# Memory attention, tanhshrink and maxout on one core: g three steps ahead instead of two

## The chip, the core and the metric

The kernel runs on one core of one Trainium2 chip. The time is device microseconds (us) of one execution. A core has TensorE (PE, matmuls), VectorE (DVE), ScalarE (ACT), GpSimd (POOL) and SyncE (SP), which issues most of the DMAs; each works through its own queue of instructions in order, and they wait for one another through semaphores.

## The reference

All inputs come as 64-bit floats. There are 8 batches of 576 tokens, 4608 tokens in all, with 8 heads of width 64.

```python
a = softmax(phi, axis=seq)                       # phi: 32 memory slots per head
k_m, v_m = a^T k, a^T v                          # 32 x 64 per head
x = softmax(q k_m^T / 8) v_m                     # back to 4608 x 512
h = x @ w_in                                     # 512 -> 2048
g = h - tanh(h)
x2 = g @ w_out                                   # 2048 -> 512
m = max(x2 @ w1, x2 @ w2, x2 @ w3)               # 512 -> 768
out = m @ w_out2                                 # 768 -> 512
```

## The kernel before

Every product is made of three matmuls on pairs (the value rounded to the matmul's format, and the rest), by the helper `mm3` (lines 93 to 96). So every weight is first split into such a pair from its 64-bit input by `conv` (lines 116 to 143): one ScalarE step, five VectorE steps, then POOL and ScalarE for the two halves.

Attention and the first layer are merged. For each batch, `phi_gen` and `kv_mm` build the memory keys and values, `vw_gen` multiplies the memory values with a quarter of w_in into the weight tile `vw`, and `q_gen` gives the attention probabilities `at`. h is then the product of `vw` and `at`.

The main loop has 200 steps in two phases, each phase with half of the 2048 inner columns. A step is one chunk of 128 inner columns (8 to a phase) for one tile of 288, 320 or 512 tokens; a tile of 512 spans two batches. `emit_h` computes h of a step into one of two PSUM banks, `emit_g` applies tanh (ScalarE, line 453), subtracts from h in PSUM (VectorE, line 454), rounds (ScalarE, line 456) and takes the rest (POOL, line 457) into a tile `gh`. `emit_x` multiplies `gh` with a chunk of w_out and adds up in four PSUM banks; the last step of a tile adds or copies them to `xo` (lines 485 and 487) and stores that. `LG` is the lookahead: while step i is multiplied, g of step i + LG is made after the first quarter of the products, and h of step i + LG + 1 after the last.

Attention, weight conversion and the like stand in two tracks, `fg` and `bg`, one after another in each. `slot()`, called five times per step, takes some pieces from each; a piece can have a gate, the step from which it may be taken. If `emit_h` or `emit_x` needs something that isn't out yet, `need` empties the track up to it. This gives the order of emission. The order in which an engine really executes comes from the framework's scheduler, which runs a timeline of its own and prefers what was emitted first among what is ready; a thing can run long before or after its neighbours in the code.

After the two phases comes the last stage: nine tiles of 512 tokens. For each, `emit_max` makes six chunks j of the three maxout products (216 matmuls in all) with weights `wb[j]`, and `emit_out` multiplies the maxima with w_out2 (72 matmuls). `wb[0]` and `wb[1]` are converted during phase 1, stored to DRAM, and loaded (line 611) into the pool `pre`, which takes the room of phase 0's w_out. `wb[2]` is loaded the same way (line 631) into the pool `wb`, which takes the room of the two phases' tiles; `wb[3]` to `wb[5]` and the six `wz` are converted while the first tiles of the stage run.

Of the kernel before, what the change touches and what calls it, by code (L numbers as in the profile page):

```python
# [7 lines left out]
F32 = mybir.dt.float32  # L8
F32R = mybir.dt.float32r
# [13 lines left out]
def kernel(  # L23
# [23 lines left out]
    V, S, G, T, DMA = nc.vector, nc.scalar, nc.gpsimd, nc.tensor, nc.sync  # L47
    B, H, NS, D = q.shape
    M = phi.shape[3]
    P = 128  # L50
# [6 lines left out]
    KD = DM // P  # L57
    FQ = 512
    NT = 512
    NX = B * NS // NT  # L60
    LG = 2
    AHEAD = 20
    FC = 8
    J = 6

    def pool(name, space=None, stack=ctx, **kw):
        if space is not None:
            kw["space"] = space
        if space is not DRAM:
            kw["reuse_waits"] = "tile"  # L70
        return stack.enter_context(tc.tile_pool(name=name, bufs=1, **kw))
# [8 lines left out]
    ga_p = pool("ga", stack=main)  # L80
    cv_p = pool("cv", stack=main)
    at_p = pool("at", stack=main)
    attn = ExitStack()
    ap = pool("attn", stack=attn)
# [5 lines left out]
    def f(x):  # L90
        return x.bitcast(F32)

    def mm3(o, w, x, start, stop):
        T.matmul(o, w[0], x[0], start=start, stop=False)  # L94
        T.matmul(o, w[0], x[1], start=False, stop=False)  # L95
        T.matmul(o, w[1], x[0], start=False, stop=stop)  # L96
# [5 lines left out]
    def bank(i, shape, name):  # L102
        return ps_m.tile(shape, F32, tag=f"m{i}", bufs=1, name=name)
# [11 lines left out]
    def conv(src, hi, lo=None):  # L115
        raw = cv[0].tile([P, 512, 2], U32, tag="raw", bufs=2, name="raw")
        u = src.bitcast(U32)
        DMA.dma_start(out=raw.rearrange("p (k c) t -> p k (c t)", k=u.shape[1]) if len(u.shape) == 3 else raw.rearrange("p c t -> p (c t)"), in_=u)
        yield
        yield  # L120
        a = cv[0].tile([P, 512], U32, tag="cva", bufs=2, name="cva")
        b = cv[0].tile([P, 512], U32, tag="cvb", bufs=2, name="cvb")
        hw, lw = raw[:, :, 1], raw[:, :, 0]
        S.activation(f(a), f(hw), AF.Abs)
        yield
        V.tensor_scalar(f(a), f(a), TINY, HUGE, ALU.max, ALU.min)
        V.tensor_scalar(b, a, 3, 0x3FFFFFF8, ALU.logical_shift_left, ALU.bitwise_and)
        yield
        V.scalar_tensor_tensor(out=b, in0=hw, scalar=0xC0000000, in1=b, op0=ALU.bitwise_and, op1=ALU.bitwise_or)  # L129
        yield  # L130
        V.tensor_scalar(a, b, 0xFF800000, None, ALU.bitwise_and)
        V.scalar_tensor_tensor(out=f(a), in0=lw, scalar=2.0 ** -52, in1=f(a), op0=ALU.mult, op1=ALU.mult)
        yield
        if lo is None:
            G.tensor_add(hi, f(b), f(a))
            yield
            return
        G.tensor_add(f(a), f(b), f(a))
        x = f(a).rearrange("p (k c) -> p k c", k=hi.shape[1]) if len(hi.shape) == 3 else f(a)
        S.copy(hi, x)  # L140
        yield
        G.tensor_sub(lo, x, f(hi))  # L142
        yield
# [13 lines left out]
    def load_phi(b):  # L157
        if b < B and b not in phi_t:
            t = ap.tile([P, H, C, M], F32, tag="phi", bufs=1, name="phi")
            DMA.dma_start(out=t[:, :, :4], in_=phi[b, :, :4 * P].rearrange("h (p c) m -> p h c m", p=P))  # L160
            DMA.dma_start(out=t[:64, :, 4], in_=phi[b, :, 4 * P:].rearrange("h p m -> p h m"))
            G.memset(t[64:, :, 4], -3e38)
            phi_t[b] = t
# [22 lines left out]
    def phi_gen(b):  # L186
        load_phi(b)
        ph = phi_t.pop(b)
        yield
        mx = ap.tile([P, H, M], F32, tag="mx", bufs=1, name="mx")  # L190
        V.tensor_reduce(mx, ph.rearrange("p h c m -> p h m c"), axis=AX.X, op=ALU.max)
        yield
        pm = bank(1, [P, 2, 2, P], "ps_mx")
        for i in range(2):
            T.transpose(pm[:, 0, i], mx[:, 4 * i:4 * i + 4].rearrange("p h m -> p (h m)"), ident)
        mt = ap.tile([P, 2], F32, tag="mt", bufs=1, name="mt")
        V.tensor_reduce(mt, pm[:, 0], axis=AX.X, op=ALU.max)
        yield
        dg = ap.tile([P, 2, P], F32, tag="dg", bufs=1, name="dg")
        V.tensor_tensor(out=dg, in0=ident[:, None, :].to_broadcast([P, 2, P]), in1=mt[:, :, None].to_broadcast([P, 2, P]), op=ALU.mult)  # L200
        T.matmul(pm[:, 1].rearrange("p i j -> p (i j)"), ones, dg.rearrange("p i j -> p (i j)"), start=True, stop=True)
        yield
        freed[1] = V.tensor_tensor(out=ph, in0=ph, in1=pm[:, 1].rearrange("p i (h m) -> p (i h) m", m=M)[:, :, None, :].to_broadcast([P, H, C, M]), op=ALU.subtract).ins
        yield
        S.activation(ph, ph, AF.Exp)
        yield
        ph_t[b] = ph
        yield
# [39 lines left out]
    def kv_gen(b):  # L248
        yield from phi_gen(b)
        yield from kv_mm(b)  # L250
# [93 lines left out]
    JP = 3  # L344
    wb_d = [dram.tile([P, 3, KD, 2, P], F32, name=f"wb_d{j}") for j in range(JP)]

    def wb_conv(w, j, t=None):
        o = cv_p.tile([P, KD, 2, P], F32R, tag="cs", bufs=1, name="cs") if t is None else t[:, w]
        src = (moe2_w1, moe2_w2, moe2_w3)[w]
        yield from conv(src[:, j * P:(j + 1) * P].rearrange("(k p) c -> p k c", p=P), o[:, :, 0], o[:, :, 1])  # L350
        if t is None:
            DMA.dma_start(out=wb_d[j][:, w], in_=f(o))
            yield
# [34 lines left out]
    fg, bg = Track(), Track()  # L388
    now, cnt, rate = [0], [0], [10, 8]

    def slot():
        cnt[0] += 1
        for i, tr in enumerate((fg, bg)):
            for _ in range((cnt[0] * rate[i]) // 4 - ((cnt[0] - 1) * rate[i]) // 4):
                tr.step(now[0])
# [53 lines left out]
    def emit_g(i):  # L449
        ps = h_t.pop(i)  # L450
        nt = steps[i][1][1]
        th = ga_p.tile([P, NT], F32, tag="th", bufs=2, name="th")[:, :nt]
        S.activation(th, ps, AF.Tanh)  # L453
        V.tensor_sub(th, ps, th)  # L454
        gh = ga_p.tile([P, 2, NT], F32R, tag="gh", bufs=3, name="gh")[:, :, :nt]
        S.copy(gh[:, 0], th)  # L456
        G.tensor_sub(gh[:, 1], th, f(gh[:, 0]))  # L457
        g_t[i] = gh
# [6 lines left out]
    def emit_x(i):  # L465
# [13 lines left out]
        for dm in range(KD):  # L479
            mm3(emit_x.ps[dm], (wt[:, 0, dm * P:(dm + 1) * P], wt[:, 1, dm * P:(dm + 1) * P]),  # L480
                (gh[:, 0], gh[:, 1]), first, final)
            if final:
# [3 lines left out]
                else:  # L486
                    (S.copy if dm % 2 else V.tensor_copy)(xo[:, dm], ps)
            if dm == 0 and i + LG < len(steps):
                emit_g(i + LG)
            slot()  # L490
# [5 lines left out]
    def run(lo, hi):  # L496
        for i in range(lo, hi):
# [3 lines left out]
            emit_x(i)  # L501
            if i + LG + 1 < len(steps):
                emit_h(i + LG + 1)
            slot()
# [34 lines left out]
    for ph in range(2):  # L539
        for b in range(B):  # L540
            s0, bb = start[ph, b], ph * B + b
            order += [(bb, 0), (bb, 1)] if bb > 1 else []
            aq = max([s0 - AHEAD + 4] + [last_u[bb - 3, fq] - LG for fq in range(2) if bb > 2])
            av0, av1 = (max(s0 - d, last_u[order[2 * bb + fq - 4]] - LG) if bb > 1 else 0 for fq, d in enumerate((8, 6)))
            if ph == 0 and b > 1:
# [34 lines left out]
    wo_s.close()  # L580
    last = ExitStack()
    pre_p = pool("pre", stack=last, side="right")
    wb = [pre_p.tile([P, 3, KD, 2, P], F32R, name=f"wb{j}") for j in range(2)]
    x_t = {}
    xh_p = [pre_p]

# [20 lines left out]
    def pre():  # L607
        while bg.q:
            bg.step(10 ** 9)
        for j in range(2):  # L610
            G.dma_start(out=wb[j], in_=wb_d[j])
        load_x(0)

    hooks[start[2, 0] - 14] = [pre]
# [7 lines left out]
    wb_p = pool("wb", stack=last2)  # L622
# [2 lines left out]
    cv[0] = b_p  # L625
    ps_b = pool("ps_b", PSUM, last2)
    wz = []
    for j in range(2, J):
        wb.append(wb_p.tile([P, 3, KD, 2, P], F32R, name=f"wb{j}"))
        if j < JP:  # L630
            G.dma_start(out=wb[j], in_=wb_d[j])
        else:
            for w in range(3):
                bg.add(("wb", j), wb_conv(w, j, wb[j]))
    for j in range(J):
        wz.append(wb_p.tile([P, 2, DM], F32R, name=f"wz{j}"))
        bg.add("wz", wz_conv(j, wz[j]))
# [3 lines left out]
    def emit_max(i, j):  # L641
        xh = x_t[i]
        pss = []
        bg.need_all(("wb", j))
        for w in range(3):
            for _ in range(LR):
                bg.step(10 ** 9)
            ps = ps_b.tile([P, NT], F32, tag=f"w{w}", bufs=2, name=f"ps_w{w}")
            for kc in range(KD):
                mm3(ps, (wb[j][:, w, kc, 0], wb[j][:, w, kc, 1]), (xh[:, 0, kc], xh[:, 1, kc]), kc == 0, kc == KD - 1)  # L650
            pss.append(ps)
        m = b_p.tile([P, NT], F32, tag="m", bufs=2, name="m")
        S.copy(m, pss[0])
        V.tensor_max(m, pss[1], m)  # L654
        V.tensor_max(m, pss[2], m)
        mh = b_p.tile([P, 2, NT], F32R, tag="mh", bufs=12, name="mh")
        S.copy(mh[:, 0], m)  # L657
        G.tensor_sub(mh[:, 1], m, f(mh[:, 0]))  # L658
        m_t[i, j] = mh
# [59 lines left out]
```

## Time and profile before

| | us |
|---|---|
| median of 3 timed runs | 1469.13 |
| lowest and highest | 1468.34, 1474.32 |
| the profiled execution | 1464.11 |
| its span | 1462.4 |
| TensorE busy in it | 1359.7 |
| VectorE busy in it | 637.0 |
| POOL busy in it | 450.9 |
| ScalarE busy in it | 418.6 |

The span runs from the first to the last instruction that the profile shows. Durations are those of the one profiled execution. Matmuls overlap, so their pace is read from the distance of two starts and not from the duration of one. The first product of phase 1 starts at 524.0 us, phase 1 ends at 849 us, and the last stage takes the rest.

### The profile page before, as it was taken

The page shows a single profiled execution, that of the slowest core. Times are in us where ns is not written, and L with a number is a line of the kernel's source. Part 1 is how long each engine was busy: PE and PEld are TensorE (multiplying, and loading weights), DVE is VectorE, ACT ScalarE, POOL GpSimd, SP SyncE. Part 2 cuts the span into 40 slices and gives each one's busy share as a digit, 9 for nine tenths or more (in the row PEclk, how much of TensorE's full clock was granted, in tenths as well). Part 3 has the DMA queues.
Part 4 walks back from the last instruction along what each step waited for, and adds up shares of the span by engine and source line. Part 5 has one row for each costly group of instructions (what it writes and reads, how often), then busy time and mean ns, then how long its engine had stood idle before and what let it go on. Part 6 is the DMA issues. An engine that isn't in the chain of part 4 may idle for free.

```text
span 1462.4 us, 21348 instructions
## 1 busy us (share of the span) xinstructions
PE 1359.7 (93%) x8672; PEld 1128.9 (77%) x8672; DVE 637.0 (44%) x1013; ACT 418.6 (29%) x805; POOL 450.9 (31%) x399
## 2 busy tenths in 40 slices
PE   2576898999998999999999999899999999999998
PEld 1354786887886888888889987788888888888886
DVE  3889977446538773323223269621212121121110
ACT  1334334344334443433333233311111111111110
POOL 0446554334325663232223345511111111111110
PEclk9687999999999999999999999999999999999999
DMA  8565887535615583413221242210101011110001
GB/s 203 155 195 145 234 256 216 136 116 134 159 68 209 185 271 128 144 67 111 66 80 56 88 164 87 87 44 15 43 15 49 17 43 30 37 29 15 15 15 44
DMA packets 177970, 152.39 MB, mean 104 GB/s; under 512 B 94160, under 2 KB 153552, under 8 KB 176464
## 3 DMA queue, kind: packets, MB, share of 16 engines
q1 hardware_dynamic: 177440, 146.31, 33.5%
q0 software_dynamic: 432, 4.72, 1.0%
q8 instruction: 68, 1.11, 0.3%
q14 instruction: 30, 0.25, 0.1%
HBM read 101.97 MB, written 49.02 MB: 103 GB/s over the span
## 4 chain that ended last, share of the span: by engine, by line
PE 72%; DVE 12%; DMA 5%; SPq 4%; issue 3%; POOL 2%; ACT 1%; DVEq 0%; POOLq 0%; ACTq 0%
PE ps_w L96 9%; PE ps_w L95 9%; PE ps_w L94 9%; PE ps_x L94 7%; PE ps_x L95 7%; PE ps_x L96 7%; PE ps_h L94 4%; PE ps_h L96 4%; PE ps_h L95 4%; PE ps_o L95 3%; PE ps_o L96 3%; PE ps_o L94 3%; SPq L181 2%; PE ps_w L106 2%; DVE cvb L129 2%
## 5 line engine op out<-in xcount | busy, mean ns | idle before, releaser
L457 POOL TENSOR_TENSOR gh<-th,gh 128x320 fp32r<-128x320 f32 (+2 forms) x200 | 204.3, 1023 | 348.0 <-ACT gh L456 329.2
L95 PE MATMUL ps_x<-gh,wo 128*128 128x320 f32 (+2 forms) x800 | 267.4, 336 | 1.5 <-POOL gh L457 1.5
L94 PE MATMUL ps_x<-gh,wo 128*128 128x320 f32 (+2 forms) x800 | 255.4, 338 | 10.3 <-DVE xo L485 4.2
L96 PE MATMUL ps_x<-gh,wo 128*128 128x320 f32 (+2 forms) x800 | 263.9, 333 | 0.5 <-POOL wo L142 0.5
L94 PE MATMUL ps_w<-xh,wb 128*128 128x512 f32 x648 | 255.4, 394 | 3.5 <-ACT wb L140 3.5
L95 PE MATMUL ps_w<-xh,wb 128*128 128x512 f32 x648 | 255.7, 395 | 0.0
L96 PE MATMUL ps_w<-xh,wb 128*128 128x512 f32 x648 | 255.3, 395 | 0.0
L658 POOL TENSOR_TENSOR mh<-m,mh 128x512 fp32r<-128x512 f32 x54 | 71.5, 1324 | 446.0 <-ACT mh L657 445.9
L454 DVE TENSOR_TENSOR th<-ps_h,th 128x320 f32<-128x320 f32 (+2 forms) x200 | 106.9, 536 | 223.1 <-ACT th L453 222.8
L94 PEld LDWEIGHTS ps_x<-gh,wo 128*128 128x128 f32 x800 | 148.7, 191 | 37.4 <-issue 17.8
L94 PE MATMUL ps_h<-at,vw 128*128 128x320 f32 (+2 forms) x512 | 159.7, 313 | 18.0 <-ACT at L297 9.9
L95 PEld LDWEIGHTS ps_x<-gh,wo 128*128 128x128 f32 x800 | 152.4, 190 | 18.9 <-issue 7.2
L96 PEld LDWEIGHTS ps_x<-gh,wo 128*128 128x128 f32 x800 | 152.0, 190 | 11.0 <-issue 0.9
L96 PE MATMUL ps_h<-at,vw 128*128 128x320 f32 (+2 forms) x512 | 155.9, 306 | 1.5 <-DVE vw L317 1.5
L95 PE MATMUL ps_h<-at,vw 128*128 128x320 f32 (+2 forms) x512 | 155.8, 304 | 0.0
L453 ACT ACTIVATE th<-ps_h 128x320 f32<-128x320 f32 (+2 forms) x200 | 94.8, 477 | 208.5 <-PE ps_h L96 198.6
L94 PEld LDWEIGHTS ps_w<-xh,wb 128*128 128x128 f32 x648 | 122.5, 189 | 31.8 <-ACT wb L140 4.3
L456 ACT CAST gh<-th 128x320 fp32r<-128x320 f32 (+2 forms) x200 | 99.9, 500 | 162.7 <-DVE th L454 150.0
L654 DVE TENSOR_TENSOR m<-ps_w,m 128x512 f32<-128x512 f32 x54 | 37.3, 690 | 246.2 <-PE ps_w L96 246.2
L95 PEld LDWEIGHTS ps_w<-xh,wb 128*128 128x128 f32 x648 | 122.5, 189 | 27.9
L96 PEld LDWEIGHTS ps_w<-xh,wb 128*128 128x128 f32 x648 | 122.4, 189 | 27.6 <-POOL wb L142 0.3
L94 PEld LDWEIGHTS ps_h<-at,vw 128*128 128x128 f32 x512 | 100.4, 196 | 41.4 <-DVE th L454 17.1
(83 smaller groups left out, 1694.1 us busy)
## 6 DMA issues: line engine op xcount, KB each, us to landing
raw<-in_moe_w_out_dram SPq DMA_DIRECT2D x22, 512.0 KB, 3.4
qt<-in_q_dram SPq DMA_DIRECT2D x128, 72.0 KB, 2.8
at_d<-at SPq DMA_DIRECT2D x16, 576.0 KB, 3.5
at<-at_d SPq DMA_DIRECT2D x8, 1152.0 KB, 5.0
raw<-in_moe_w_dram SPq DMA_DIRECT2D x18, 512.0 KB, 3.6
xr<-xd SPq DMA_DIRECT2D x36, 256.0 KB, 2.8
out_dram<-ob SPq DMA_DIRECT2D x144, 64.0 KB, 1.7
xd<-xo SPq DMA_DIRECT2D x14, 640.0 KB, 3.5
```

Of the source, the lines that this page charges most:

```text
L94: T.matmul(o, w[0], x[0], start=start, stop=False)
L95: T.matmul(o, w[0], x[1], start=False, stop=False)
L96: T.matmul(o, w[1], x[0], start=False, stop=stop)
L106: ins = [T.matmul(o, w, x, start=True, stop=True).ins for o, w, x in mms]
L129: V.scalar_tensor_tensor(out=b, in0=hw, scalar=0xC0000000, in1=b, op0=ALU.bitwise_and, op1=ALU.bitwise_or)
L181: DMA.dma_start(out=t[64 * e + 32 * h:64 * e + 32 * h + 32, r], in_=src[e, h, r])
L453: S.activation(th, ps, AF.Tanh)
L454: V.tensor_sub(th, ps, th)
L456: S.copy(gh[:, 0], th)
L457: G.tensor_sub(gh[:, 1], th, f(gh[:, 0]))
L654: V.tensor_max(m, pss[1], m)
L658: G.tensor_sub(mh[:, 1], m, f(mh[:, 0]))
```

## The change

`LG` becomes 3, and `gh` gets four buffers in place of three. The diagonal tile `dg` of `phi_gen` takes the buffer of `mx`. The weights of the last stage become one tile for each j and each of the three products, (j, w), instead of one for each j. Five of them, (0, 0) to (1, 1), are loaded into `pre` in phase 1; (1, 2) is loaded at the start of the last stage, ahead of (2, 0) to (2, 2).

```diff
-    LG = 2
+    LG = 3
...
-        dg = ap.tile([P, 2, P], F32, tag="dg", bufs=1, name="dg")
+        dg = ap.tile([P, 2, P], F32, tag="mx", bufs=1, name="dg")
...
-        gh = ga_p.tile([P, 2, NT], F32R, tag="gh", bufs=3, name="gh")[:, :, :nt]
+        gh = ga_p.tile([P, 2, NT], F32R, tag="gh", bufs=4, name="gh")[:, :, :nt]
...
-    wb = [pre_p.tile([P, 3, KD, 2, P], F32R, name=f"wb{j}") for j in range(2)]
+    wb = {(j, w): pre_p.tile([P, KD, 2, P], F32R, name=f"wb{j}{w}") for j, w in ((0, 0), (0, 1), (0, 2), (1, 0), (1, 1))}
...
-        for j in range(2):
-            G.dma_start(out=wb[j], in_=wb_d[j])
+        for j, w in wb:
+            G.dma_start(out=wb[j, w], in_=wb_d[j][:, w])
...
-    for j in range(2, J):
-        wb.append(wb_p.tile([P, 3, KD, 2, P], F32R, name=f"wb{j}"))
-        if j < JP:
-            G.dma_start(out=wb[j], in_=wb_d[j])
-        else:
-            for w in range(3):
-                bg.add(("wb", j), wb_conv(w, j, wb[j]))
+    for j in range(1, J):
+        for w in range(3):
+            if (j, w) not in wb:
+                wb[j, w] = wb_p.tile([P, KD, 2, P], F32R, name=f"wb{j}{w}")
+                if j < JP:
+                    G.dma_start(out=wb[j, w], in_=wb_d[j][:, w])
+                else:
+                    bg.add(("wb", j), wb_conv(w, j, wb[j, w]))
...
-                mm3(ps, (wb[j][:, w, kc, 0], wb[j][:, w, kc, 1]), (xh[:, 0, kc], xh[:, 1, kc]), kc == 0, kc == KD - 1)
+                mm3(ps, (wb[j, w][:, kc, 0], wb[j, w][:, kc, 1]), (xh[:, 0, kc], xh[:, 1, kc]), kc == 0, kc == KD - 1)
```

## Rows read from the trace of the kernel before

**Rows 1.** Stretches: length, busy us (instructions) of each engine, TensorE's granted clock, DMA share, GB/s.
```profile
40.00:120.00 80.00, 47.18 (x410) 31.58 (x406) 66.81 (x109) 25.27 (x49) 36.35 (x31) 0.70 0.64 168
120.00:260.00 140.00, 121.48 (x1129) 102.36 (x1122) 116.47 (x196) 59.78 (x128) 75.41 (x70) 0.94 0.74 217
...
440.00:520.00 80.00, 72.10 (x444) 58.66 (x442) 63.61 (x96) 34.63 (x66) 48.71 (x38) 0.96 0.61 213
520.00:849.00 329.00, 328.91 (x2137) 290.37 (x2138) 109.96 (x194) 117.13 (x234) 111.36 (x109) 1.00 0.31 107
...
880.00:920.00 40.00, 36.52 (x149) 28.63 (x148) 37.23 (x47) 13.37 (x23) 23.78 (x18) 0.96 0.29 96
```

**Rows 2.** Waits of TensorE: who waited for whom, us in total, times, longest.
```profile
PE ps_h L94 <- DVE th L454: 7.4, 16, 1.3
...
PE ps_x L94 <- ACT gh L456: 1.9, 2, 1.6
PE ps_x L95 <- POOL gh L457: 1.5, 4, 0.6
```

**Rows 3.** Timeline of TensorE near 117 us: start, us, operation, idle before and its end.
```profile
117.50 0.85 PE L94 MATMUL ps_h<-at,vw 128*128 128x288 f32 x2 [9.88 <-ACT at L297]
```

**Rows 4.** Timeline of TensorE where batches 3, 5 and 7 enter.
```profile
254.30 0.44 PE L195 MATMUL ps_mx<-ident,mx 128*128 128x128 f32 x2 [2.39 <-DVE vw L317]
...
353.67 0.44 PE L195 MATMUL ps_mx<-ident,mx 128*128 128x128 f32 x2 [1.60 <-DVE vw L317]
...
456.76 1.92 PE L106 MATMUL ps_w<-wi,vT 64*32 64x512 f32 x4 [4.80 <-POOL wi L135]
```

**Rows 5.** Timeline of VectorE where batch 7 enters.
```profile
451.50 1.78 DVE L129 SCALAR_TENSOR_TENSOR cvb<-raw,cvb 128x512 uint32<-128x512 uint32 x1
...
456.53 1.28 DVE L454 TENSOR_TENSOR th<-ps_h,th 128x512 f32<-128x512 f32 x2
```

**Rows 6.** Timelines of ScalarE, POOL and VectorE at the end of phase 1.
```profile
845.73 0.67 ACT L124 ACTIVATE cva<-raw 128x512 f32<-128x512 f32 x1
...
846.73 0.57 POOL L631 DMA_DIRECT2D wb<-wb_d  x1
855.31 1.67 POOL L138 TENSOR_TENSOR cva<-cvb,cva 128x512 f32<-128x512 f32 x1 [8.01 <-DVE cva L132]
...
848.71 1.69 DVE L485 TENSOR_TENSOR xo<-ps_x,xo 128x320 f32<-128x320 f32 x4 [3.38 <-PE ps_x L96]
850.32 0.42 DVE L126 TENSOR_SCALAR cva<-cva 128x512 f32<-128x512 f32 x1
```

**Rows 7.** Timeline of TensorE in the last stage: its two longest waits.
```profile
894.98 0.80 PE L94 MATMUL ps_w<-xh,wb 128*128 128x512 f32 x1 [2.75 <-ACT wb L140]
...
928.71 0.74 PE L94 MATMUL ps_o<-wz,mh 128*128 128x512 f32 x1 [3.38 <-ACT wz L140]
```

**Rows 8.** Timeline of TensorE: eight starts in a row of a product with 320 columns.
```profile
848.22 0.31 PE L95 MATMUL ps_x<-gh,wo 128*128 128x320 f32 x1
...
849.25 0.31 PE L96 MATMUL ps_x<-gh,wo 128*128 128x320 f32 x1
```

**Rows 9.** Weight loads: the page's DMA line (KB, us to landing), durations of issues (min/median/max).
```profile
wb<-wb_d POOLq DMA_DIRECT2D x3, 1536.0 KB, 7.7
...
L611 POOL DMA_DIRECT2D wb<-wb_d x2: 567/644/720, 525.9 to 540.8; - x2
```

**Rows 10.** Timeline of TensorE in the last stage: two stretches of five starts.
```profile
862.12 0.39 PE L96 MATMUL ps_w<-xh,wb 128*128 128x512 f32 x1
...
863.03 0.39 PE L94 MATMUL ps_w<-xh,wb 128*128 128x512 f32 x1
...
878.13 0.39 PE L96 MATMUL ps_w<-xh,wb 128*128 128x512 f32 x1
...
879.06 0.39 PE L94 MATMUL ps_w<-xh,wb 128*128 128x512 f32 x1
```

More of the change, by code (lines that the diff above doesn't have):

```diff
@@ L347, in wb_conv @@
     def wb_conv(w, j, t=None):
-        o = cv_p.tile([P, KD, 2, P], F32R, tag="cs", bufs=1, name="cs") if t is None else t[:, w]
+        o = cv_p.tile([P, KD, 2, P], F32R, tag="cs", bufs=1, name="cs") if t is None else t
         src = (moe2_w1, moe2_w2, moe2_w3)[w]
```

## The prediction

> **What bounds the kernel now.** I read the busy time by stretch first. TensorE is the engine to watch: it is never idle for long from 520 to 849 us (0.1 us in 329), while from 40 to 120 us it is idle for 32.8 of 80 us, from 120 to 260 us for 18.5 of 140, from 440 to 520 us for 7.9 of 80, from 880 to 920 us for 3.5 of 40 [rows 1]. In the stretches with idle time VectorE is the busy one: 66.8 of 80 us, 116.5 of 140, 63.6 of 80, 37.2 of 40, and only 110 of 329 where TensorE is full [rows 1]. So the middle and most of the last stage are a stream of matmuls that no lookahead shortens; the change can move only the idle time in the four other stretches, which sums to 62.7 us, and the half-speed clock around it (granted clock 0.70 and 0.94 in the first two stretches, 0.96 in the two later ones).
>
> Then the waits of TensorE, to see which idle time a longer lookahead touches. Products that wait for g cost 1.9 + 1.5 us in all. h waits 7.4 us, 16 times, for the subtraction that reads its PSUM bank out [rows 2]. The long waits are for something else: 9.88 us for the attention output of batch 1 at 117.50 us [rows 3], and 2.39, 1.60 and 4.80 us at 254.30, 353.67 and 456.76 us [rows 4]. These three lie where the second batch of a group of two (batches 3, 5, 7) enters; the attention track is serial, so that batch's chain is emitted in the slots of the few steps just ahead. The timeline of VectorE there shows the backlog: conversion work (1.78 us for one L129) stands ahead of two tanhshrink subtractions, which start only at 456.53 us [rows 5].
>
> Last, the end of phase 1 and the last stage. ScalarE turns from the last g to the first conversion at 845.73 us, POOL issues the load of the third weight at 846.73 us, VectorE idles 3.38 us, takes the four adds of the last tile at 848.71 us and begins the conversion only at 850.32 us [rows 6]. That conversion chain is then what the last stage waits for: 2.75 us at 894.98 us, 3.38 us at 928.71 us [rows 7].
>
> **The change, part by part.** All sums are against the profiled execution, 1464.11 us with a span of 1462.4 us; the median of the three timed runs, 1469.13 us, is 5.0 us above it, and I add that at the end.
>
> *Lookahead and fourth g buffer.* No matmul, activation or subtraction is added; every h and every g stands one step earlier in the order in which the scheduler weighs instructions. A g has one more step, at least 12 + 6 matmuls at 0.147 us = 2.6 us (0.147 us is 1.03 us over seven starts [rows 8]), before it is needed. At most the 1.9 + 1.5 us of waits for g go [rows 2]; what is late next where they go is the same VectorE queue, through h's wait for its bank. I take half, -0.8, with 0 and -3.4 as ends. The 7.4 us of h's own waits stay: h of step k uses the bank of step k-2 under both depths, because PSUM keeps two buffers for it.
>
> *The 9.88 us at 117.50 us.* By my count of the products in the trace, all those of the first two tiles are over when it begins. TensorE has nothing that a lookahead could bring, and the chain that ends it is emitted by the same slots as before: 0 as the middle.
>
> *The three entries of a second batch.* Two effects of opposite sign. The attention slots hang on the products; one h more is done before them, so the chain may begin one h step later: 6 x 0.147 = 0.88 us, at most 12 x 0.147 = 1.76 us where a tile spans two batches, three times, +5.3 us at most. Against it, the first g of the new batch is ranked one step, that is five slots of attention and conversion work, earlier on VectorE, whose backlog is what TensorE then waits for; all of 2.39 + 1.60 + 4.80 = 8.8 us is the most that this can give. The lead is rebuilt in idle time, where an h costs nothing, so I think the second effect a little stronger: -1.0, ends +5.3 and -8.8.
>
> *The end of phase 1.* The last h is followed by four product steps, not three, so the last g is out one product step earlier: 12 x 0.147 = 1.76 us [rows 8]. ScalarE's first conversion step and POOL's load follow it at once [rows 6], so both start 1.8 us earlier. Whether VectorE uses it depends on whether the scheduler now puts the conversion ahead of the four adds. If it does not, nothing is won. If it does, up to the 3.38 us idle time before them is used, and since VectorE is busy for 37.2 of 40 us afterwards, the lead lasts until TensorE's 3.5 us of waits before 920 us are gone [rows 1], with up to 1.6 us of clock that a shorter wait may save (an estimate from the granted 0.96 of that stretch: 0.04 x 40 us). I take -1.8, ends 0 and -5.1.
>
> *Weights as single tiles.* Three POOL loads become nine: five in phase 1 for two, four at the start of the last stage for one. One issue takes 0.57 to 0.72 us [rows 6, 9], so six more are 3.4 to 4.3 us of POOL. Half of it falls in phase 1, where TensorE loses 0.1 us in 329 [rows 1], half after the last g, where POOL idles 8.01 us until 855.31 us [rows 6]. If that cover were gone, the first conversion would start at most 3 x 0.72 = 2.2 us later. A POOL load that waits for its data or its room holds up whatever g stands behind it, and TensorE would see that within a step; in phase 1 the stores of these weights come first, and each load is now tied to one store instead of three, so I count nothing. The weight that is loaded later is needed at 863.03 us [rows 10]. Its issue ends near 846 us, and even with the time that a transfer of three times the size takes, a median of 7.7 us [rows 9], it is there by 854 us: 9 us to spare. The conversions of the last stage write three small tiles in place of a third of one large; that frees them from waiting for room that only a sibling needs, and I count 0.
>
> *The diagonal in the room of the maximum.* It is written after a reduction that itself waits for both transposes of the maximum, and the next maximum comes a whole batch later. No wait is added: 0, and nothing that a queue could lose.
>
> *Placement.* The 512-column matmuls of the last stage run at two paces, 0.91/4 = 0.228 us between 862.12 and 863.03 us and 0.93/4 = 0.233 us between 878.13 and 879.06 us [rows 10]. The faster one is seen with weights and moving operand on one side of SBUF, the slower across. The weight that moves sides changes 12 matmuls in each of nine tiles, five one way and four the other: +0.1 us.
>
> Sum: -0.8 + 0 - 1.0 - 1.8 + 0.1 = -3.5 us, so 1460.6 us for the profiled execution and 1465.6 us for the median. The ends are +5.4 and -17.2.
>
> A rule speaks for more. The same gap that comes again on the engine that should be full can mean that there is no room for the next tile, in the Trainium skill's page Perfetto Trace Analysis, section Optimization Strategy, put in my words. By that rule a fourth buffer removes the repeated gaps, and the time is that of the first rival. The rows agree that gaps repeat, but they name PSUM banks and VectorE, not g's buffers.
>
> **The rivals.**
> *Depth cures the repeated gaps* (faster). With g one step ahead everywhere, VectorE's queue no longer reaches TensorE: 7.4 + 3.4 us of waits go [rows 2], and the end of phase 1 gives its 1.8. 1464.1 - 12.6 + 5.0 = 1456.5 us. For it: 16 short h waits, all after a late subtraction. Against it: PSUM still has two banks for h.
> *The lead displaces the attention chain* (slower). At the start and at the three entries the chain begins one h later, up to 1.76 us, and one more subtraction, 1.28/2 = 0.64 us [rows 5], stands ahead of it on VectorE. Four places at 2.4 us: +9.6, so 1478.7 us. It decides from about 1.8 us lost per place (7.3 us in all). For it: VectorE is 83% busy from 40 to 260 us [rows 1]. Against it: an h done in idle time costs nothing.
> *The change does not do what it says.* Two PSUM banks hold h back, and the order of execution hardly differs: 1469 us.
> *Placement.* All later tiles move by up to 4 KB. If the pace depends on finer addresses than the side, some half of the 2592 matmuls of the last stage (nine tiles of 216 + 72) changes by 0.005 us: 6.5 us either way, 1459 or 1472 us around the forecast.
>
> **How the numbers follow.** The forecast has 0.48, the cure by depth 0.23, displacement 0.14, no effect 0.10, placement 0.05. What a measurement of this kernel can tell from no change is about 0.5%, 7.3 us: under 1461.8 or over 1476.5 us. The forecast's spread puts about 0.07 of it below that, the first rival nearly all of its share, displacement about 0.11 above. Faster 0.29, same 0.56, slower 0.15. The range is 1455 to 1477 us: it takes in the first rival and most of the way to displacement.
>
> **What would show it.** Right: waits for g near zero, h's waits for its bank still near 7 us; the 9.88 us still there; the first conversion on VectorE before 849 us and TensorE's waits between 880 and 950 us shorter by 2 us or more; nine POOL loads of about 0.6 us with no wait of a product behind them. Wrong: the idle time between 40 and 260 us changes by more than 5 us in either direction, since I hold the order of the attention chain to be unchanged; or TensorE waits for a weight between 860 and 870 us.

## The result and the profile after

The changed kernel is slower: 1478.24 us as the median of 8 runs (1474.11 to 1481.4), against 1469.47 us for the kernel before (8 runs, 1466.91 to 1474.32). The ratio is 1.0059, with a 95% interval of 1.0043 to 1.0074, so 6 to 11 us. The forecast of 1465.6 us has the wrong sign, and the range ended 1.2 us too low. The profiled execution of after took 1474.56 us, 10.4 us more than that of before, which was faster than all eight timed runs of before; after's is the second fastest of its eight.

The stretches of after, with the columns of [rows 1]:

```profile
40.00:120.00 80.00, 46.60 (x402) 32.26 (x408) 68.96 (x108) 25.40 (x49) 37.39 (x31) 0.73 0.63 165
120.00:260.00 140.00, 117.33 (x1092) 98.85 (x1077) 113.39 (x191) 56.90 (x122) 74.81 (x67) 0.90 0.71 209
440.00:520.00 80.00, 71.81 (x462) 59.35 (x461) 66.50 (x97) 32.88 (x63) 44.34 (x36) 0.94 0.52 182
520.00:849.00 329.00, 327.66 (x2137) 289.19 (x2136) 116.08 (x199) 118.73 (x237) 116.14 (x114) 1.00 0.31 107
880.00:920.00 40.00, 37.16 (x151) 29.02 (x150) 39.14 (x44) 13.52 (x22) 25.46 (x19) 0.96 0.33 102
```

The loss lies early: from 120 to 260 us TensorE is busy for 117.3 us where it was for 121.5, at a granted clock of 0.90 where it was 0.94. Not all of this is the change: f1 (told of below), whose time equals before's, is busy for 119.3 us there at 0.92. The waits of TensorE in after (who waited for whom, us, times, longest) show what replaced what:

```profile
PE ps_h L94 <- DVE th L454: 11.6, 10, 2.3
PE ps_h L94 <- ACT at L297: 11.5, 2, 10.8
...
PE ps_h L96 <- DVE vw L317: 5.0, 3, 1.9
...
PE ps_h L94 <- ACT vw L315: 2.3, 2, 1.7
```

No product waits for g any more; those 3.4 us are gone [rows 2]. But h waits 11.6 us for its bank where it was 7.4 us, and 5.0 us for its weight `vw` in three places. Part of the longer bank waits would be there without the change: they are 9.6 us in f1.

A better measure than fixed windows is when the product of a given step starts on TensorE. Each figure is the start in the profile of that kernel less the start in the profile of before, in us (f1, f3, h1 and h2 are told of below; f1 has a lead of two throughout, f3 of three from step 8, h2 from step 4, h1 everywhere but in steps 4 to 7):

```
step (start before)  f1    f3    h2    h1   after
   0 (66.0)         -0.8   0.0  -0.4   1.8  -0.1
   8 (129.3)        -0.3   0.5   0.6   5.0   3.9
  24 (194.7)         2.4   6.7   7.7  16.0  12.8
  56 (323.7)         2.9   2.7   2.3  13.4   7.6
  68 (380.2)         3.7   7.0   6.2  16.4  10.8
  88 (461.8)         3.4   6.8   6.0  15.0   9.4
  96 (496.1)         4.5  10.6  10.2  19.1  12.8
 112 (550.4)         5.0  10.3  10.7  18.4  12.6
 199 (847.6)         4.8   7.7   8.1  15.8  10.0
```

About 3 us of each column from step 24 on is the fast profile of before: f1, whose time hardly differs from before's, is 2.9 us behind at step 56 too. And 1.8 us of h1's column are there at the first product already. Beyond that, after loses some 5 us by step 56, and, against f1, 2.4 and 2.3 us more where batch 5 (steps 56 to 68) and batch 7 (88 to 96) enter. In phase 1, steps 112 to 199, 2.6 us come back, in f1 0.2.

**The start in detail.** TensorE in after while the memory keys and values of batch 1 are built (start, us, operation, idle before and its end):

```profile
76.23 0.30 PE L222 MATMUL ps_kv<-ones,phi 128*32 128x1 f32 x14
77.29 0.61 PE L94 MATMUL ps_h<-at,vw 128*128 128x288 f32 x1 [0.76 <-ACT at L297]
77.83 0.68 PE L222 MATMUL ps_kv<-ones,phi 128*32 128x1 f32 x22
78.85 0.61 PE L95 MATMUL ps_h<-at,vw 128*128 128x288 f32 x1 [0.34 <-POOL at L298]
...
80.56 2.52 PE L226 MATMUL ps_kv<-kv,phi 128*32 128x128 f32 x40
...
90.13 0.66 PE L242 MATMUL ps_t<-ident,n 128*64 128x128 f32 x8 [1.76 <-DVE n L236]
```

The h of step 4, now emitted a step earlier, runs inside these products and waits twice for the attention probabilities `at` of its tile; the small products behind it wait with it. VectorE of after then comes to the finished keys and values (`rc`, then `n`) late:

```profile
82.43 0.43 DVE L127 TENSOR_SCALAR cvb<-cva 128x512 uint32<-128x512 uint32 x1
...
84.59 0.44 DVE L454 TENSOR_TENSOR th<-ps_h,th 128x288 f32<-128x288 f32 x1
84.95 0.41 DVE L131 TENSOR_SCALAR cva<-cvb 128x512 uint32<-128x512 uint32 x1
85.40 0.69 DVE L132 SCALAR_TENSOR_TENSOR cva<-raw,cva 128x512 f32<-128x512 uint32 x1
86.12 0.92 DVE L126 TENSOR_SCALAR cva<-cva 128x512 f32<-128x512 f32 x1
87.07 1.40 DVE L127 TENSOR_SCALAR cvb<-cva 128x512 uint32<-128x512 uint32 x1
88.39 0.15 DVE L233 TENSOR_SCALAR rc<-ps_kv 128x2 f32<-128x2 f32 x1
...
89.57 0.42 DVE L236 TENSOR_TENSOR n<-ps_kv,rc 128x256 f32<-128x256 f32 x1
```

TensorE's last products of this kind in before, and VectorE's `rc` and `n`:

```profile
77.70 2.52 PE L226 MATMUL ps_kv<-kv,phi 128*32 128x128 f32 x40
...
85.14 0.15 DVE L233 TENSOR_SCALAR rc<-ps_kv 128x2 f32<-128x2 f32 x1
...
86.07 0.42 DVE L236 TENSOR_TENSOR n<-ps_kv,rc 128x256 f32<-128x256 f32 x1
```

In both kernels the products are over some 5 us before `rc` starts (80.22 and 85.14 us in before, 83.08 and 88.39 us in after). So it is the order of VectorE's queue that sets the start of `n`, and not the end of the products. VectorE of h2 (a lead of two in steps 0 to 3), which reaches the same point with less ahead of it:

```profile
84.39 0.43 DVE L131 TENSOR_SCALAR cva<-cvb 128x512 uint32<-128x512 uint32 x1
84.73 0.15 DVE L233 TENSOR_SCALAR rc<-ps_kv 128x2 f32<-128x2 f32 x1
...
85.65 0.42 DVE L236 TENSOR_TENSOR n<-ps_kv,rc 128x256 f32<-128x256 f32 x1
```

Counted from the first product of step 0 to `n`, VectorE does 15 conversion instructions of 14.2 us in before, f1, f3 and h2, and `n` starts 20.1 us after that product. In after and h1 there are 19 of 17.6 us and one subtraction more, and `n` comes after 23.7 us. It is the head of the attention chain of batch 1, whose end h of step 8 waits for:

```profile
118.80 0.85 PE L94 MATMUL ps_h<-at,vw 128*128 128x288 f32 x2 [10.78 <-ACT at L297]
...
128.29 1.96 PE L106 MATMUL ps_w<-wi,vT 64*32 64x512 f32 x16 [4.05 <-DVE vw L317]
```

Here 1.3 us of the 3.5 are left [rows 3], since the chain's later links come closer together. But two more conversion instructions (eight, not six) stand between `at` and the copy of `vw` that the second of these waits is for, and the product of step 8 starts 3.9 us late. The same wait in before:

```profile
125.99 1.38 PE L106 MATMUL ps_w<-wi,vT 64*32 64x512 f32 x16 [3.04 <-DVE vw L317]
```

**The end of phase 1.** ScalarE, POOL and VectorE of after, beside [rows 6]:

```profile
853.94 0.67 ACT L124 ACTIVATE cva<-raw 128x512 f32<-128x512 f32 x1
...
854.94 2.16 POOL L633 DMA_DIRECT2D wb<-wb_d  x4
...
858.39 1.68 DVE L485 TENSOR_TENSOR xo<-ps_x,xo 128x320 f32<-128x320 f32 x4 [4.85 <-PE ps_x L96]
859.99 0.42 DVE L126 TENSOR_SCALAR cva<-cva 128x512 f32<-128x512 f32 x1
```

ScalarE's conversion step does start earlier: 3.7 us ahead of the last product step, against 1.9 before. VectorE leaves it lying, idles 4.85 us and takes the four adds first, as before. So the last stage gains next to nothing; its two waits, beside [rows 7], on TensorE:

```profile
904.42 0.50 PE L94 MATMUL ps_w<-xh,wb 128*128 128x512 f32 x1 [2.22 <-ACT wb L140]
...
938.48 0.79 PE L94 MATMUL ps_o<-wz,mh 128*128 128x512 f32 x1 [4.54 <-ACT wz L140]
```

### The profile page after: what moved, and what is told of

It reads as the page before. It is cut to its first block, busy times and chain, and to the rows that moved or that the text cites. A ratio compares the mean times of both kernels' runs of the same rounds, so it can differ in the third digit from the quotient of the medians.

```text
span 1472.8 us, 21350 instructions
## 1 busy us (share of the span) xinstructions
PE 1363.1 (93%) x8672; PEld 1135.1 (77%) x8672; DVE 649.3 (44%) x1013; ACT 419.1 (28%) x805; POOL 458.0 (31%) x405
## 4 chain that ended last, share of the span: by engine, by line
PE 69%; DVE 13%; DMA 6%; SPq 5%; issue 3%; ACT 2%; POOL 2%; DVEq 0%; POOLq 0%; ACTq 0%
PE ps_w L96 9%; PE ps_w L95 9%; PE ps_w L94 9%; PE ps_x L94 7%; PE ps_x L95 6%; PE ps_x L96 6%; PE ps_o L94 3%; PE ps_h L94 3%; PE ps_o L95 3%; PE ps_o L96 3%; PE ps_h L96 3%; PE ps_h L95 3%; SPq L181 3%; DVE cvb L129 2%; DVE cva L131 2%
## 5 line engine op out<-in xcount | busy, mean ns | idle before, releaser
L94 PE MATMUL ps_x<-gh,wo 128*128 128x320 f32 (+2 forms) x800 | 268.9, 341 | 4.8 <-DVE xo L487 2.6
L95 PE MATMUL ps_x<-gh,wo 128*128 128x320 f32 (+2 forms) x800 | 268.4, 336 | 0.0
L96 PE MATMUL ps_x<-gh,wo 128*128 128x320 f32 (+2 forms) x800 | 266.6, 335 | 0.5 <-POOL wo L142 0.5
L94 PE MATMUL ps_h<-at,vw 128*128 128x320 f32 (+2 forms) x512 | 160.5, 314 | 25.6 <-DVE th L454 11.6
L94 PEld LDWEIGHTS ps_x<-gh,wo 128*128 128x128 f32 x800 | 153.8, 194 | 34.3 <-issue 13.5
L96 PEld LDWEIGHTS ps_x<-gh,wo 128*128 128x128 f32 x800 | 153.1, 192 | 12.7 <-issue 2.4
L95 PEld LDWEIGHTS ps_x<-gh,wo 128*128 128x128 f32 x800 | 153.9, 192 | 9.0 <-issue 2.2
```

## The experiments

Sixteen kernels ran, each timed in several rounds against the kernel before on the same chip. Ratios are to before, with 95% intervals; times are medians. Where the lead varies by step, the emission is this, with `lead(i)` as given at each run:

```diff
-            if dm == 0 and i + LG < len(steps):
-                emit_g(i + LG)
+            while dm == 0 and ng[0] < min(nh[0], i + lead(i) + 1, len(steps)):
+                emit_g(ng[0])
+                ng[0] += 1
...
-            if i + LG + 1 < len(steps):
-                emit_h(i + LG + 1)
+            while nh[0] < min(i + lead(i) + 2, len(steps)):
+                emit_h(nh[0])
+                nh[0] += 1
```

Before step 0 as many h and g are emitted as `lead(0)` asks for.

### First: which part of the change, and where

**e1_parts_lg2**: after, but the lead of before.

```diff
-    LG = 3
+    LG = 2
```

> The changed kernel with the lookahead set back to two steps; the fourth g buffer, the diagonal in the maximum's room and the weights as single tiles stay. Theory (the longer lookahead displaces the attention chain at the start): the loss is gone, 1469 us within 4, and the first product of step 8 starts near 129 us as before the change (133 us after it). Rival (the moved tiles, the split weights or nine POOL loads cost it): still near 1478 us. Second rival (any disturbance of the order costs that much, because the order before was a lucky one): somewhere between, 1473 us or more, with the loss at other places.

1475.56 us, 1.0038 [1.0026, 1.005]. The theory missed; this is the second rival's time. So the buffers and the single-tile weights without the lead are not free. Its profile falls 5.0 us behind in steps 104 to 112, where a wait of ScalarE is longer than in before (4.62 us, not 2.8). All five loads of phase 1 leave POOL within 3.9 us; SyncE's store of a converted weight is held up behind a load of `xo`; ScalarE's next rounding waits for that store, and the tanhshrink steps queue behind it. POOL, SyncE and ScalarE of e1:

```profile
529.40 2.32 POOL L611 DMA_DIRECT2D wb<-wb_d  x4
...
532.77 0.57 POOL L611 DMA_DIRECT2D wb<-wb_d  x1
...
542.00 0.59 SPq L478 DMA_DIRECT2D xo<-xd  x1
542.64 8.38 SPq L352 DMA_DIRECT2D wb_d<-cs  x2
...
548.72 0.62 ACT L140 CAST cs<-cva 128x512 fp32r<-128x512 f32 x1 [4.62 <-DMA wb_d<-cs]
```

TensorE is busy for 36.3 us of the 40 from 520 to 560 us there, in f1 for 39.2. The bunch of loads alone does not explain it: in f1 four of the five leave POOL within 2.3 us and ScalarE waits 3.27 us for such a store, at no cost. And of the 3.7 us in which e1's TensorE is idle there, only 1.75 us come after the wait of 4.62 us.

**e2_lg3_buf3**: after with three g buffers.

```diff
-        gh = ga_p.tile([P, 2, NT], F32R, tag="gh", bufs=4, name="gh")[:, :, :nt]
+        gh = ga_p.tile([P, 2, NT], F32R, tag="gh", bufs=3, name="gh")[:, :, :nt]
```

> The changed kernel with three buffers for g in place of four: h and g are still ranked three steps ahead, but a g can't be written before the product three steps back is over. Theory (rank alone displaces the chain; h of step 4 among the first kv products): near 1478 us, with the same h between the kv products at 77 us. Rival (it is the fourth buffer that lets g crowd VectorE): near 1469 us.

1480.77 us, 1.007 [1.0056, 1.0084]. With a lead of three the fourth buffer is worth about 0.1%, which the overlapping intervals do not show to be there.

**e3_lg3_from32**: after, `lead(i)` is 2 to step 31, then 3.

> The changed kernel with lookahead two up to step 31 and three from step 32 on, where phase 0's second half of the batches begins. Theory (the cost is in the start, steps 0 to 56, 7.6 us of 10.4 in the traces; 2 us more at the entry of batch 5): 1470 to 1473 us. If the longer lookahead costs at every entry of a second batch, as the prediction's slower rival had it, 1474 us or more. Rival (tiles and loads): 1478 us.

1470.81 us, 1.0016 [1.0006, 1.0026].

**e4_lg3_until32**: after, `lead(i)` is 3 to step 31, then 2.

> The changed kernel with lookahead three up to step 31 and two from step 32 on: the counterpart. Theory (the cost is in the start): 1475 to 1478 us, with step 8 near 133 us and step 32 about 6 us later than before the change. If the entries carry it: 1471 us or less.

1484.06 us, 1.0103 [1.0089, 1.0118], more than either theory. With e1 and after these two make a square: three in the first 32 steps costs (1.03 + 0.59 - 0.16 - 0.38) / 2 = 0.54%, and behind them it is 0.33% better than the lead of two with the same buffers.

### Second: the parts on the kernel before

**f1_weights_only**: before with the single-tile weights alone, loads and uses as in the change.

```diff
-    wb = [pre_p.tile([P, 3, KD, 2, P], F32R, name=f"wb{j}") for j in range(2)]
+    wb = {(j, w): pre_p.tile([P, KD, 2, P], F32R, name=f"wb{j}{w}") for j, w in ((0, 0), (0, 1), (0, 2), (1, 0), (1, 1))}
...
```

> The kernel before with the weights of the last stage as single tiles, (1, 2) loaded in the last stage; lookahead two, three g buffers and the diagonal's own room stay. The lookahead-two version of the changed kernel took 1475.6 against 1469.3 us, so the tiles or the fourth buffer cost 6 us without any lookahead. Theory (five POOL loads in a bunch near 530 us fill the DMA queues, a store comes out late, ScalarE waits 4.6 us for its buffer, the products stop): 1474 to 1477 us, with that wait in the trace between 535 and 555 us. Rival (the fourth g buffer costs it, by letting g crowd VectorE at the start): 1469 us.

1470.87 us, 1.0007 [0.9995, 1.0019]: nothing, so the theory missed.

**f2_before_lead3_from32**: before, with three g buffers, `lead(i)` is 2 to step 31, then 3.

> The kernel before, nothing else changed, with lookahead three from step 32 on and still three g buffers. With the tiles, lookahead three from step 32 took 1470.8 and lookahead two 1475.6 us. Theory (behind the start the longer lookahead wins some 4 to 5 us by covering the hiccups near 500 to 560 us): 1464 to 1467 us, faster than both. Rival (it only repairs what the bunched loads break): 1469 us or a little more, with 2 to 4 us lost at the entry of batch 5 (step 64).

1471.67 us, 1.0018 [1.0007, 1.0028]. The gain that the theory wanted did not come.

**f3_lg3_from8**: after, `lead(i)` is 2 to step 7, then 3.

> The changed kernel with lookahead two up to step 7 and three from step 8 on, the step that starts batch 1. Theory (what costs at the start is h of step 4 among the kv products of batch 1 and the chain behind it): like lookahead three from step 32, 1470 to 1472 us. Rival (lookahead three costs through all of the VectorE-bound start, steps 8 to 31 as well): 1475 to 1479 us.

1473.64 us, 1.0029 [1.0018, 1.004], between the two. Half of the loss goes with the first eight steps.

**f4_before_ahead22**: before, with the attention of later batches gated two steps earlier, as a measure of what any other order costs.

```diff
-    AHEAD = 20
+    AHEAD = 22
```

> The kernel before with the attention of later batches allowed two steps earlier (22 instead of 20). It changes the order of a few hundred instructions and has nothing to do with the change; it shows how much any disturbance of the order costs. Theory (the losses have places and causes): within 3 us of 1469. Rival (the order before is a lucky one, and any other costs 5 us and more): 1474 us or more.

1474.8 us, 1.004 [1.0027, 1.0053], the rival's time. An edit that has nothing to do with the lead moves the time by 0.4%; a difference of that size can't be told from a merely different order by its size alone.

### Third: is it the h inside batch 1's products?

**g1_chain_first**: after, with thirteen pieces of the attention track emitted ahead of h of step 4.

```diff
+            if i == 0:
+                for _ in range(13):
+                    fg.step(0)
             if i + LG + 1 < len(steps):
```

> The changed kernel in which, in step 0 only, 13 more pieces of the attention track are emitted ahead of h of step 4, so that the whole kv product of batch 1 is ranked before it again; lookahead three stays everywhere. Theory (h of step 4 inside the kv product costs some 5 us at the start): 1472 to 1474 us, as with lookahead three from step 8 (1473.6), and the kv product in one piece again near 77 us. Rival (lookahead three in the first steps costs through g on VectorE or ScalarE, whatever the rank of the kv product): 1477 us or more. Second rival (any order is worth plus or minus 5 us): anything.

1477.11 us, 1.0059 [1.004, 1.0078]. A miss. The products of keys and values run in one piece again, with 15 conversions and 20.1 us up to `n`; yet from `n` on the chain takes longer, h of step 8 starts at 119.97 us, and the product of step 56 is 9.4 us behind. So the loss does not need the split products. What g1 has in common with after is the end of the chain: eight conversions before the second copy of `vw`, and a long wait for it on TensorE:

```profile
129.42 1.96 PE L106 MATMUL ps_w<-wi,vT 64*32 64x512 f32 x16 [4.91 <-DVE vw L317]
```

**g2_before_chain_first**: the same edit on before.

> The kernel before with the same 13 pieces emitted earlier in step 0. If the attention chain of batch 1 bounds the start by its rank, the 9.88 us of waiting at 117 us get shorter: 1464 to 1467 us. Rival (VectorE's conversions bound it, and the rank of the chain gives nothing more): 1468 to 1470 us, or slower by up to 5 us as any other disturbance.

1469.44 us, 1.0008 [0.9996, 1.002]: the edit by itself is harmless.

**g3_chain_all**: g1 with the gates of attention and of `vw` a step earlier as well.

```diff
-    AHEAD = 20
+    AHEAD = 21
...
-            av0, av1 = (max(s0 - d, last_u[order[2 * bb + fq - 4]] - LG) if bb > 1 else 0 for fq, d in enumerate((8, 6)))
+            av0, av1 = (max(s0 - d, last_u[order[2 * bb + fq - 4]] - LG) if bb > 1 else 0 for fq, d in enumerate((9, 7)))
```

> The changed kernel with the attention chain moved along with the lookahead at all places: the 13 pieces in step 0, and for the later batches all gates one step earlier (21 in place of 20, 9 and 7 in place of 8 and 6). Theory (the lookahead also costs 2 to 4 us at the entries of batches 5 and 7, because the chain stays where it was): the entries cost no more than with lookahead two, 1468 to 1471 us. Rival (the entries lose to the disturbed order as such): 1473 us or more.

1484.23 us, 1.0112 [1.0095, 1.013]: worse, and a miss. Moving the whole chain a step ahead along with h does not restore the old order.

**g4_before_lead3_until8**: before, three g buffers, `lead(i)` is 3 to step 7, then 2.

> The kernel before, nothing else changed, with lookahead three in steps 0 to 7 only. Theory (these steps alone cost about 5 us): 1473 to 1476 us, with h of step 4 among the kv products of batch 1. Rival (they cost only together with the fourth buffer or the moved tiles): 1468 to 1470 us.

1476.65 us, 1.0057 [1.004, 1.0074]. Eight of 200 steps with a longer lead, and nothing else of the change, cost as much as all of it.

### Fourth: which of the eight steps, h or g

**h1_lg2_in_4to7**: after, `lead(i)` is 2 in steps 4 to 7 alone.

> The changed kernel with a lead of three everywhere but in steps 4 to 7, where it is two, so that h of step 8 comes where the kernel before has it; steps 0 to 3 stay as in the changed kernel (ratio 1.0059, product of step 56 7.6 us behind the profile before). Theory 'early half': the cost is made in steps 0 to 3, ratio 1.005 to 1.007, step 56 at +7 to +10. Rival 'late half': it is made by h of step 8, ratio 1.002 to 1.0035 as with lead three from step 8 only (1.0029), step 56 at +2 to +4, and the wait of h for at near 9.7 us.

1480.49 us, 1.0079 [1.0059, 1.0098], a little above the early half's range.

**h2_lg2_in_0to3**: after, `lead(i)` is 2 in steps 0 to 3, then 3.

> The changed kernel with a lead of two in steps 0 to 3 and three from step 4, so that only h of step 8 and what follows come a step earlier. Theory 'early half': ratio 1.002 to 1.0035, step 56 at +2 to +4, kv's products in one piece and n near 86 us. Rival 'late half': ratio 1.005 to 1.007, step 56 at +7 to +10, and the wait of h for at above 10.5 us. If both halves cost some, this run and the one with two in steps 4 to 7 lie both at 1.004 to 1.0055.

1474.88 us, 1.0039 [1.0026, 1.0052]. With f3 (two in both halves) and after (three in both) these make a square. Three in steps 0 to 3 costs (0.79 + 0.59 - 0.39 - 0.29) / 2 = 0.35%, with an interval of about 0.15 either way; three in steps 4 to 7 costs (0.59 + 0.39 - 0.79 - 0.29) / 2 = -0.05%, which is nothing. It is the early half, 5 us. The interval holds the noise of the times alone and not what a merely different order costs (f4). The wait of h of step 8 for `at` points the same way, but decides nothing, since e1 with its lead of two waits 10.9 us too (TensorE of h2, then of h1, from 60 to 200 us):

```profile
PE ps_h L94 <- ACT at L297: 10.0, 1, 10.0
```

```profile
PE ps_h L94 <- ACT at L297: 11.7, 2, 10.9
```

**h3_g_later_until8**: after with every h in its place (`lead(i)` is 3), but g at the lead of two to step 7, and one g fewer before step 0.

```diff
-            while dm == 0 and ng[0] < min(nh[0], i + lead(i) + 1, len(steps)):
+            while dm == 0 and ng[0] < min(nh[0], i + (2 if i < 8 else 3) + 1, len(steps)):
```

> The changed kernel with every h where it has it, but each g of steps 0 to 10 computed one step later, where the kernel before has it. If the h's place on TensorE and the attention work that it calls for is what costs, ratio 1.005 to 1.007 and step 56 at +7 to +10. Rival: the g's ahead of the conversions and of attention on VectorE cost it, ratio 1.002 to 1.0035, step 56 at +2 to +4.

1478.52 us, 1.0063 [1.0046, 1.008], as after. In these steps it is the place of the h's, not the g's.

**h4_before_lead1_until8**: before, `lead(i)` is 1 to step 7, then 2.

> The kernel before with a lead of one in steps 0 to 7 and two from there. Theory 'each step of lead costs at the start': the product of step 8 starts 1 to 4 us earlier than in the kernel before and the ratio is 0.996 to 0.999. Rival 'g needs the cover': x of the first eight steps waits for its g on ScalarE and GpSimd, up to 1.5 us in each, and the ratio is 1.002 to 1.008. If the two cancel, 0.999 to 1.002.

1474.71 us, 1.0042 [1.0026, 1.0059]. The shorter lead does shorten the chain: h of step 8 starts at 112.52 us after 5.6 us of wait, 5.0 us earlier than in before (2.6 of which were there at the first product already), and its product 3.9 us earlier. Then it gives this back and more between steps 20 and 24 (5.4 us ahead, then 9.2 us behind). TensorE of h4 from 60 to 230 us:

```profile
PE ps_h L94 <- DVE th L454: 12.5, 8, 3.2
PE ps_mx L195 <- DVE vw L317: 6.2, 1, 6.2
PE ps_h L94 <- ACT at L297: 5.6, 1, 5.6
```

Neither theory is the whole: the second and the third step of lead do delay the attention chain, but without the second h waits 12.5 us for its bank (6.0 us in before), and the transposes (`ps_mx`) of a later batch wait 6.2 us for VectorE's copy of `vw`. Of one, two and three steps at the start, two is the best.

**All eighteen kernels by their lead in steps 0 to 3.** The conversions are those of VectorE between `at` and the second copy of `vw`, as in the start in detail above; the last two columns give the time in us from the product of step 0 to that of step 8 and of step 56, each in the profile of that kernel.

| lead | kernels | ratio to before | conversions | to step 8 | to step 56 |
|---|---|---|---|---|---|
| three | after, e2, e4, g1, g3, g4, h1, h3 | 1.0057 to 1.0112 | 8 in each | 66.5 to 68.4 | 265.4 to 271.0 |
| two | before, e1, e3, f1, f2, f3, f4, g2, h2 | 1 to 1.0040 | 6 in each | 63.3 to 64.5 | 257.7 to 261.7 |
| one | h4 | 1.0042 | 6 | 62.0 | 269.1 |

No kernel of the first row is as early at these steps as any of the second, whatever else was edited. So the loss at the start is not that of just any different order, and g1 is no exception. That the two conversions are what costs was not tried by itself.

No kernel beats before: f1 and g2 equal it within their intervals, and all others are slower.

## Why the prediction was wrong

**The step that failed: "the chain that ends it is emitted by the same slots as before: 0 as the middle."** The slots are the same, but the h's stand elsewhere among them, and VectorE's order changes with that. The step looked at what TensorE could do during the 9.88 us and asked whether h of step 8 had work to overtake. What costs is the lead of three in steps 0 to 3: with it eight conversions and not six stand before the copy of `vw` at the chain's end, and the product of step 8 starts 2 us and more later after that of step 0. The term was 0 and measures 5 us (0.35 ± 0.15%, from the square of four kernels); on the kernel before, with three to step 7, it measures 8 us (g4). In after the chain's head is late too, since h of step 4 runs inside the products that begin it and four more conversions go past on VectorE; g1 loses as much without that. The bounds did not hold the term either, as this place had none: the text gave the entries of batches 3, 5 and 7 an end of +5.3 and the start nothing; only the slower rival priced it, at 2.4. The idle time from 40 to 260 us, which was to show this step wrong if it changed by over 5 us, grew from 51.3 to 56.1 us, just short of that. It could not have told: in f1, which costs nothing, it is 55.3 us. The starts of the steps show it better.

**The entries of batches 3, 5 and 7: -1.0 forecast, and the sign was wrong.** Lead three from step 32 on before's buffers (f2) costs 0.18%, 2.6 us for all that follows step 32, inside the end of +5.3. "The lead is rebuilt in idle time, where an h costs nothing" is what fails: h at the longer lead arrives before its weight and then waits where other work waited in before. TensorE of before at the three entries, ahead of [rows 4], then of after:

```profile
245.00 0.39 PE L96 MATMUL ps_h<-at,vw 128*128 128x256 f32 x1 [0.55 <-DVE vw L317]
...
349.45 0.39 PE L96 MATMUL ps_h<-at,vw 128*128 128x256 f32 x1 [0.93 <-DVE vw L317]
...
450.43 1.09 PE L106 MATMUL ps_w<-wi,vT 64*32 64x512 f32 x16 [0.95 <-DVE vw L317]
```

```profile
255.35 0.39 PE L96 MATMUL ps_h<-at,vw 128*128 128x256 f32 x1 [1.94 <-DVE vw L317]
...
355.77 0.39 PE L94 MATMUL ps_h<-at,vw 128*128 128x256 f32 x1 [1.65 <-ACT vw L315]
...
357.75 0.58 PE L96 MATMUL ps_h<-at,vw 128*128 128x256 f32 x1 [1.20 <-DVE vw L317]
...
363.35 0.69 PE L195 MATMUL ps_mx<-ident,mx 128*128 128x128 f32 x2 [1.33 <-DVE vw L317]
...
460.14 0.39 PE L96 MATMUL ps_h<-at,vw 128*128 128x256 f32 x1 [1.82 <-DVE vw L317]
...
466.67 1.92 PE L106 MATMUL ps_w<-wi,vT 64*32 64x512 f32 x4 [4.11 <-POOL wi L135]
```

With [rows 4] the waits come to 2.9, 2.5 and 5.8 us in before and to 1.9, 4.2 and 5.9 us in after. From 230 to 520 us, h's waits for `vw` grew from 1.5 to 6.7 us, but those of the other products for it fell from 4.9 to 1.3 us. So the waits mostly changed their place, and no gain came of it.

**Waits for g: -0.8 forecast.** All 3.4 us of them went, and "h's own waits stay" did not hold: 7.4 became 11.6 us, 4.2 more (2.2 of these 4.2 us are in f1 as well). The text had said what would be late next, the same queue through h's bank, and allowed for it by "I take half"; half of 3.4 is 1.7 and not 0.8, and at either size the term had the sign wrong.

**End of phase 1: -1.8 forecast, nothing gained.** ScalarE's lead of 1.8 us came as worked out. The condition that the text named, VectorE taking the conversion ahead of the adds, was not met, and the text took it as met for its middle. The last stage took 0.4 us longer than in before's profile.

**Weights as single tiles: right.** f1 says 0.07% [-0.05, 0.19]. Nine POOL loads (0.55 and 0.60 us on the mean), no product waits behind them, and TensorE does not wait for a weight between 860 and 870 us. Alone with the new buffers, though (e1), a store that comes out late holds up ScalarE for 4.62 us; "each load is now tied to one store" did not price that. Which of the two buffer edits makes the difference between f1 and e1 was not tried.

**Placement: +0.1 forecast, and its mechanism is borne out.** In after the matmuls of weight (1, 2) start 0.234 us apart in the five tiles whose moving operand lies in the pool that the weight left, where they were 0.227 us apart in before; in three of the four others they went from 0.234 to 0.227 us, in one to 0.230 us.

**The rivals.** The time is that of displacement (1478.7 us), and its mechanism is near the one found: the chain's links stand later on VectorE. That its sum is met within 0.5 us is luck, since it is not four places at 2.4 us each: one place makes 5 us or more, and all that follows step 32 makes 2.6 us (f2). Its chance of 0.14 was too low for a reason that [rows 1] held ready: VectorE is busy for 83% of the time from 40 to 260 us, so an h done there in TensorE's idle time still brings VectorE work that a full queue has to order. The rival of no effect (1469 us) lies outside the interval, and a pace that goes by finer addresses would show in the last stage, which took 0.4 us more. The cure by depth is refuted. It leaned on the Trainium skill, page Perfetto Trace Analysis, section Optimization Strategy, by which the same gap repeating on the engine that should be full can mean too little room for the next tile. Here more room for g and the depth removed the 3.4 us of waits for g, and TensorE waited longer for h's two PSUM banks, to which the change gave no room, and for `vw`.

**What stays open.** Why a lead of three in steps 0 to 3 makes the scheduler put two more conversions ahead of the copies of `vw`, and whether these two make all of the loss at the start. And what the rest of after's 0.59% consists of: the entries are in it, but f4 shows that an unrelated order moves as much, so a cause for each tenth of a per cent would be a story.

## What to carry to other kernels

A lookahead was not free here, where the engine that feeds it is full: a longer lead changed what stands ahead of the serial chain that ends the stage. So follow that chain from its first link to its last and ask what the longer lead puts in front of each, not only what TensorE could do during its last wait. Choose the depth by stage; one lead for all steps was set here by eight of 200 steps. And measure an unrelated reordering of the same kernel first, to know how far any order moves the time.

## What the runs showed of the hardware

The same VectorE instruction on the same shape takes very different times: L127 took 0.43 us at 82.43 us (in the rows of after above; POOL was between two instructions) and 1.40 us at 87.07 us, while POOL ran this:

```profile
86.71 1.47 POOL L135 TENSOR_TENSOR wi<-cvb,cva 128x512 f32<-128x512 f32 x1
```

It is so throughout after's trace: the 21 instructions of L127 that ran with no POOL instruction beside them took 0.41 to 0.43 us, the 35 others 0.40 to 1.64 us. So an order that moves VectorE's work under POOL's can cost it three times the undisturbed duration. That POOL is the cause was not tried by a run of its own.
